# Retention attention and two routed expert layers on one core: border by halves, first expert in sequence, last routing in steps

## The chip, the cores and the metric

One core of a Trainium2 chip runs the whole program in one launch. The metric is the device time of one execution in microseconds (us).

## What is computed

Three layers follow one another on 1536 tokens of 512 values. The reference, cut to what matters:

```python
# attention, B=2, H=8, S=768, D=64
for t in range(S):
    state = gamma * state + outer(k[:, :, t], v[:, :, t])
    y[:, :, t] = scale * einsum('bhd,bhde->bhe', q[:, :, t], state)
# first expert layer, on tokens with x @ w_skip > 0, E=8, F=1024
e_idx = argmax(xc @ w_gate); gate_w = softmax(xc @ w_gate)[e_idx]
out = x; out[do_compute] = xc + gate_w * (relu(xc @ w1[e]) @ w2[e])
# second expert layer, on all tokens, each expert up to its capacity
out[i] = gate_w[i] * (relu(x[i] @ w1[e]) @ w2[e])
```

## The kernel before

**Attention** runs over six chunks of 128 positions, for both sequences (`units`, line 529). `main` (line 661) issues scores, the running state, outputs and, between their steps, one step of routing the chunk before (`sink`, line 423): the logits, the pick of an expert (`pick`, line 282), the row numbers (`numbers`, line 405, on POOL), the tokens' rows turned back (`rows_T`, line 390), written to a table in DRAM (`write_rows`, line 335), their ranks, and one-hot matrices `where` that TensorE sums into `tab`, the table of slots (`to_slots`, line 322). The keys are scaled by decays on POOL (`scale_k`, line 570; `decays`, line 582, prepares the queries' factors `gqc`).

**Weights** come in pieces of 1 MB over SP's queue into five buffers `big` (`load_w`, line 205), in the order of the list `order`. Each is split into a high and a low part of FP32R, `hi` by ACT (line 237) and `lo` by DVE (line 240), and `pump` (line 255) issues a part of a split at each step of the program. The product of two such operands is three matmuls (`mm3`, line 757). Three split weights fit during attention, five after it.

**The border** between attention and experts is `last_chunk` (line 461). The first 128-row block of expert 0, `a0`, is gathered from the table once chunk 4's rows are written; the rows of chunk 5 that belong to it are added by one-hot products (`place`, line 352). Then come the slot sums of chunk 5, the gathers of the other experts' blocks, and the first layer.

**The first expert layer** runs over eight experts with one block each: `layer1` (line 766), then `layer2` of the expert before (line 783), with side steps (`step_side`, line 894) that route each finished block for the second expert layer (`route_b`, line 806): transposes, logits, pick, ranks, slot sums. After expert 7 its routing must be through before the blocks of the second layer can be gathered. Meanwhile block (0, 0) of the second layer, which is known earlier, is computed. The other blocks go in pairs (`pair_layer1`, `pair_layer2`), and `emit_out` (line 860) scales and scatters the results.

The order is written out by hand: each engine executes its instructions in program order, and an instruction that waits holds up all behind it on its engine or queue. PE below is TensorE, DVE VectorE, ACT ScalarE, POOL GpSimd, SP the engine whose queue issues the loads; PEld are PE's loads of the stationary operand.

## Time and profile before

| | us |
|---|---|
| median of 3 runs | 414.49 |
| range of the runs | 414.24 to 416.0 |
| the profiled execution | 413.43 |
| span of its trace | 411.6 |
| PE busy in the span | 381.8 (93%) |
| DVE, ACT, POOL busy | 247.3, 210.0, 119.4 |

The span is from the first to the last instruction; 1.8 us of the execution lie outside it. A wait in the trace is idle time of an engine together with the instruction that released it.

### The profile page before, as it was taken

How to read it: one execution, taken by the hardware profiler on the slowest of the kernel's cores; microseconds unless marked ns; L12 is line 12 of the kernel's file. 1: busy time of each engine (PE TensorE's matmuls, PEld its weight loads, DVE VectorE, ACT ScalarE, POOL GpSimd, SP SyncE). 2: the span in 40 equal slices, each digit the busy share in tenths (PEclk: the TensorE clock that was granted, in tenths of full speed). 3: DMA queues.
4: the chain of work that ended last, by engine and by line, in shares of the span. 5: the costliest groups of instructions: out<-in, count | busy, mean ns of one | idle time of the engine just before them, and what ended most of it. 6: DMA issues, size and time to landing. Idle time of an engine off the chain costs nothing.

```text
span 411.6 us, 6872 instructions
## 1 busy us (share of the span) xinstructions
PE 381.8 (93%) x2665; PEld 311.9 (76%) x2665; DVE 247.3 (60%) x440; ACT 210.0 (51%) x318; POOL 119.4 (29%) x184
## 2 busy tenths in 40 slices
PE   8879999688999999999886999999999999999993
PEld 4768778566767667766554899898989889898982
DVE  4646776549896896896652497274555637364310
ACT  1435553258776677667431665374535556354301
POOL 3665764271044043033034210311304030130202
PEclk8998999989999999999999999999999999999998
DMA  8997965749988887987963287475865657520101
GB/s 292 418 419 279 352 245 148 304 117 352 388 298 335 325 304 285 344 273 287 344 233 91 83 265 262 161 258 204 271 217 182 216 184 231 191 76 2 50 3 39
DMA packets 18336, 95.99 MB, mean 233 GB/s; under 512 B 2481, under 2 KB 2737, under 8 KB 8824
## 3 DMA queue, kind: packets, MB, share of 16 engines
q1 hardware_dynamic: 12068, 80.33, 53.6%
q0 software_dynamic: 3280, 9.76, 7.3%
q10 hardware_dynamic: 2948, 5.39, 3.5%
q8 instruction: 23, 0.38, 0.4%
q14 instruction: 17, 0.14, 0.1%
HBM read 87.03 MB, written 9.48 MB: 234 GB/s over the span
## 4 chain that ended last, share of the span: by engine, by line
PE 66%; DVE 12%; DMA 10%; ACT 6%; issue 5%; POOL 1%; SPq 0%; POOLq 0%; DVEq 0%; ACTq 0%
PE s L759 10%; PE s L761 10%; PE s L760 10%; PE o L761 7%; PE o L759 7%; PE o L760 7%; DVE lo L240 5%; DMA big<-in_w1a_dram 4%; ACT hi L237 4%; PE o L789 2%; DMA table<-rowc 2%; DVE xl L363 2%; PE m L644 2%; DMA wgt<-in_wg_dram 2%; PE m L637 1%
## 5 line engine op out<-in xcount | busy, mean ns | idle before, releaser
L240 DVE TENSOR_TENSOR lo<-big,hi 128x1024 fp32r<-128x1024 f32 (+1 forms) x126 | 145.1, 1184 | 56.0 <-ACT hi L237 55.4
L237 ACT ACTIVATE hi<-big 128x1024 fp32r<-128x1024 f32 (+1 forms) x126 | 121.8, 1014 | 3.5 <-DMA big<-in_w1a_dram 3.5
L759 PE MATMUL o<-hi,hTh 128*128 128x512 f32 x176 | 72.1, 409 | 0.3 <-ACT hTh L362 0.3
L761 PE MATMUL o<-hi,hTl 128*128 128x512 f32 x176 | 70.0, 398 | 1.0 <-DVE hTl L363 1.0
L760 PE MATMUL o<-lo,hTh 128*128 128x512 f32 x176 | 69.7, 396 | 0.0
L761 PE MATMUL s<-xh,lo 128*128 128x256 f32 x224 | 63.4, 283 | 0.0
L760 PE MATMUL s<-xl,hi 128*128 128x256 f32 x224 | 63.4, 283 | 0.0
L759 PE MATMUL s<-xh,hi 128*128 128x256 f32 x224 | 63.4, 283 | 0.0
L865 POOL DMA_INDIRECT out_dram<-y,ixo x16 | 18.2, 1137 | 142.2 <-ACT y L862 121.8
L759 PEld LDWEIGHTS s<-xh,hi 128*128 128x128 f32 x224 | 43.0, 192 | 0.3
L760 PEld LDWEIGHTS s<-xl,hi 128*128 128x128 f32 x224 | 43.0, 192 | 0.3
L761 PEld LDWEIGHTS s<-xh,lo 128*128 128x128 f32 x224 | 43.0, 192 | 0.0
L761 PEld LDWEIGHTS o<-hi,hTl 128*128 128x128 f32 x176 | 33.1, 188 | 9.7 <-DVE hTl L363 1.8
L759 PEld LDWEIGHTS o<-hi,hTh 128*128 128x128 f32 x176 | 33.1, 188 | 7.1 <-ACT hTh L362 0.5
L760 PEld LDWEIGHTS o<-lo,hTh 128*128 128x128 f32 x176 | 33.3, 189 | 6.7
L996 DVE SCALAR_TENSOR_TENSOR hTl<-s,hTh 128x512 fp32r<-128x512 f32 x28 | 19.3, 688 | 31.7 <-ACT hTh L995 31.7
L759 PE MATMUL s<-hi,xh 128*128 128x512 f32 x80 | 35.5, 444 | 2.2 <-ACT xh L362 1.3
L995 ACT ACTIVATE hTh<-s 128x512 fp32r<-128x512 f32 x28 | 16.7, 598 | 40.2 <-PE s L761 40.2
L862 ACT ACTIVATE y<-o,rowc 128x512 f32<-128x512 f32 x15 | 10.3, 689 | 47.2 <-issue 29.4
L761 PE MATMUL s<-hi,xl 128*128 128x512 f32 x80 | 32.1, 401 | 0.8 <-DVE xl L363 0.8
L760 PE MATMUL s<-lo,xh 128*128 128x512 f32 x80 | 31.9, 399 | 0.0
L842 POOL TENSOR_SCALAR rhsb<-m,cs 128x8 bf16<-128x8 bf16 x8 | 2.5, 306 | 85.2 <-DVE se L304 73.3
(151 smaller groups left out, 545.2 us busy)
## 6 DMA issues: line engine op xcount, KB each, us to landing
big<-in_w1a_dram SPq DMA_DIRECT2D x16, 1024.0 KB, 6.6
big<-in_w2a_dram SPq DMA_DIRECT2D x16, 1024.0 KB, 6.8
big<-in_w1b_dram SPq DMA_DIRECT2D x16, 1024.0 KB, 5.4
big<-in_w2b_dram SPq DMA_DIRECT2D x16, 1024.0 KB, 5.0
qk<-in_qkv_dram SPq DMA_DIRECT2D x5, 1024.0 KB, 9.8
big<-in_qkv_dram SPq DMA_DIRECT2D x5, 1024.0 KB, 6.4
table<-rowc ACTq DMA_DIRECT2D x5, 516.0 KB, 7.7
table<-row ACTq DMA_DIRECT2D x8, 258.0 KB, 4.0
```

The source lines that it names most:

```text
L237: nc.scalar.activation(out=hi[:, k], in_=r3[:, k], func=ACTF.Copy)
L240: nc.vector.tensor_tensor(out=lo[:, k], in0=r3[:, k], in1=hi[:, k].bitcast(F32), op=ALU.subtract)
L363: nc.vector.tensor_tensor(out=lo, in0=src, in1=hi.bitcast(F32), op=ALU.subtract)
L644: nc.tensor.matmul(out=o[64 * j:64 * j + 64, 128 * r:128 * r + 128], lhsT=v[:, b, 2 * r + j, :], rhs=pt[c, b][j][:, r, :], start=not c and ...
L759: nc.tensor.matmul(out=acc, lhsT=a[0], rhs=w[0], start=first, stop=False)
L760: nc.tensor.matmul(out=acc, lhsT=a[0], rhs=w[1], start=False, stop=False)
L761: nc.tensor.matmul(out=acc, lhsT=a[1], rhs=w[0], start=False, stop=last)
L789: nc.tensor.matmul(out=acc, lhsT=a[0][:, k % 4, :], rhs=w[:, k % 4, :], start=k == 0, stop=k == FT - 1)
L862: nc.scalar.activation(out=y, in_=acc, func=ACTF.Copy, scale=xs[:, GCOL + 1:GCOL + 2])
L865: new = nc.gpsimd.indirect_dma_start(out=out[:, :], out_offset=bass.IndirectOffsetOnAxis(ap=ix, axis=0), in_=y, in_offset=None, bounds_che ...
L995: nc.scalar.activation(out=hi[:, g:g + 2, :], in_=acc, func=ACTF.Relu)
L996: nc.vector.scalar_tensor_tensor(out=lo[:, g:g + 2, :], in0=acc, scalar=0.0, in1=hi[:, g:g + 2, :].bitcast(F32), op0=ALU.max, op1=ALU.subtract
```

## The change

At load, the first chunk's queries and keys come for both halves, then the values whole, then the keys by token. In attention, splits begin at chunk 2 and are issued in three steps of four, the weights of expert 0's second layer stand right behind those of its first, keys are scaled as part of the scores' step, the decays come one step earlier, and chunk rows are written to the table right after they are turned back. At the border, chunk 5's rows are placed by halves together with `a0`, both sequences' gates are made at once and their rows are written by one DMA on SP's queue; slot sums and gathers move behind the first steps of the first layer. A layer's products of two k's are ordered so that the four with the high part of the tokens come before the two with the low part (`mm3s`). Expert 0's second layer follows its first directly, and expert 1 comes after. Each block's turned tokens come after one step of the layer before, and slot sums in `route_b` come one step later. The last routing is interleaved with steps of two products of the second layer's first block, with its gate ahead of the pick, and the block's second layer then runs whole. The last output block is scaled half by ACT and half by DVE.

```diff
             nc.sync.dma_start(out=qk[:, :, b], in_=qkv[0, :, 0:2, b])
-            nc.sync.dma_start(out=kv[:, 1, b], in_=qkv[0, :, 3, b])
-        nc.sync.dma_start(out=kv[:, 0], in_=qkv[0, :, 2])
+        for i in (1, 0):
+            nc.sync.dma_start(out=kv[:, i], in_=qkv[0, :, 2 + i])
         return qk, kv
 
     grow = a_p.tile([128, 512], F32, name="grow", bufs=1)
...
         add_chunks(w1a, e, "w1a")
-        if e:
-            add_chunks(w2a, e - 1, "w2a")
+        if e != 1:
+            add_chunks(w2a, e - 1 if e else 0, "w2a")
...
             rows_T(xt, rc, 0, psum)
             if c < NCH - 2:
                 yield
             rows_T(xt, rc, 1, psum)
+            write_rows(nc.scalar, rc, B)
             yield
             rk = psum("s", 4)
             ranked(rk, lc[:, 0, :], m.rearrange("p n j -> p (n j)"), cum.rearrange("p a j -> p (a j)"))
             sl = slot(rk, m3, B)
             where = [slots_of(sl, i) for i in bs]
-            write_rows(nc.scalar, rc, B)
             for i in bs:
                 counted(m3[:, i, :])
             yield
...
+            lgs = logits(xt, [0], psum)
             yield
-            lg[0] = logits(xt, [0], psum)
+            picked(0, lgs)
             yield
-            picked(0)
-            rows_T(xt, rc, 0, psum)
-            lg[1] = logits(xt, [1], psum)
+            xr = turned_rows(xt, 0, psum)
             sl = [ranks(0)]
-            picked(1)
+            lgs = logits(xt, [1], psum)
+            nc.scalar.activation(out=rc[:, 0, 0:DM], in_=xr, func=ACTF.Copy)
+            warm(psum("s", 4), 1)
+            picked(1, lgs)
             rows_T(xt, rc, 1, psum)
-            warm(psum("s", 4), 3)
+            warm(psum("s", 4), 1)
             sl.append(ranks(1))
             acc = [psum("m"), psum("m")]
             place(acc, *late[0], True, False)
-            where = [slots_of(sl[b], 0) for b in range(B)]
-            for b in range(B):
-                gates[b]()
-                write_rows(nc.scalar, rc[:, b:b + 1, :], 1)
-            place(acc, *late[1], False, False)
-            for b in range(B):
-                to_slots(where[b], rhs[b][:, 0], 0, 16)
-            nc.vector.tensor_copy(out=ids, in_=tab)
             hi = x_p.tile([128, KT, 128], F32R, tag="xh", name="xh")
             lo = x_p.tile([128, KT, 128], F32R, tag="xl", name="xl")
+            gate(ex, B, 2, rc[:, :, GCOL:GCOL + 2])
+            write_rows(nc.sync, rc, B)
             for g in range(2):
                 ks = slice(2 * g, 2 * g + 2)
+                place(acc, *late[1], False, False, range(KT)[ks])
                 place(acc, a0, ident, False, True, range(KT)[ks])
                 split(acc[g][:, 0:256].rearrange("p (k t) -> p k t", k=2), hi[:, ks], lo[:, ks])
             x0.append((hi, lo))
-            for e in (1, 0, 2, 3):
-                xs1[e] = gather(ids[:, e:e + 1], 1 + NT)
-            for b in range(B):
-                counted(m2[b])
...
+            def gather_all():
+                where = [slots_of(sl[b], 0, sm, "whereb", 2) for b in range(B)]
+                for b in range(B):
+                    to_slots(where[b], rhs[b][:, 0], 0, 16)
+                nc.vector.tensor_copy(out=ids, in_=tab)
+                for e in (1, 0, 2, 3):
+                    xs1[e] = gather(ids[:, e:e + 1], 1 + NT)
+                for b in range(B):
+                    counted(m2[b])
+
+            x0.append(gather_all)
...
-            for g in side[0:1] if c < NCH - 1 else list(side):
+            for g in side[0:1] if c < NCH - 1 else side[::-1]:
...
             if pump and c >= 1 and (c, b) != units[-1]:
-                pump(4, count["turn"] % 3 > 0)
+                pump(4, c >= 2 and count["turn"] % 4 > 0)
...
             scale_q(c, b)
+            if b == 0 and 0 < c < NCH - 1:
+                scale_k(c)
             yield
...
+                if (c, b) == units[-1]:
+                    yield
             for r in range(4):
                 for j in range(2):
...
             o3 = o.rearrange("p (r t) -> p r t", r=4)
-            if (c, b) == units[-1]:
-                nc.vector.tensor_copy(out=xt[c][:, b], in_=o3)
-            else:
-                nc.scalar.activation(out=xt[c][:, b], in_=o3, func=ACTF.Copy)
...
                 yield from scores(c, 1)
+                if c and c + 1 < NCH:
+                    decays(c + 1)
                 if c == 0 and pump:
                     derived_late()
...
                 yield from state(c)
-            elif c + 1 < NCH:
-                decays(c + 1)
             if c + 1 < NCH:
                 yield from scores(c + 1, 0)
-                if c + 1 < NCH - 1:
-                    scale_k(c + 1)
             if c:
                 yield from outs(c, 1)
...
 
+    def mm3s(acc, pairs, first, last):
+
+        todo = [(a[0], w[i]) for a, w in pairs for i in range(2)] + [(a[1], w[0]) for a, w in pairs]
+        for i, (a, w) in enumerate(todo):
+            nc.tensor.matmul(out=acc, lhsT=a, rhs=w, start=first and i == 0, stop=last and i == len(todo) - 1)
+            if i % 2 and i < len(todo) - 1:
+                yield
+
...
         h = m_p.tile([128, FF], F32, tag="h", name="h", bufs=1)
         for j in range(2):
             acc = psum("s", 2)
             w = wt[kind, e, j]
-            for k in range(KT):
-                mm3(acc, at_k(x, k), at_k(w, k), k == 0, k == KT - 1)
-                if k == 1:
+            for k in (0, 2):
+                for _ in mm3s(acc, [(at_k(x, i), at_k(w, i)) for i in (k, k + 1)], k == 0, k == 2):
+                    if fine:
+                        yield
+                if not k:
+                    if j and parts is not None:
+                        parts.append(turned(h, 0, "hT"))
                     yield
-                if k == 2 and j and parts is not None:
-                    parts.append(turned(h, 0, "hT"))
             used((kind, e, j)) if done_with(kind, e) else None
...
             write_rows(nc.scalar, r2.unsqueeze(1), 1)
         nc.gpsimd.tensor_tensor(out=cumb, in0=cumb, in1=m, op=ALU.subtract)
-        yield from idle(2 if e < E - 1 else 1)
+        yield from idle(3 if e < E - 1 else 1)
         to_slots(where, rhs, 8, 8)
         yield
...
         y = m_p.tile([128, DM], F32, tag="y", name="y")
-        nc.scalar.activation(out=y, in_=acc, func=ACTF.Copy, scale=xs[:, GCOL + 1:GCOL + 2])
+        n = DM // 2 if shared else DM
+        nc.scalar.activation(out=y[:, 0:n], in_=acc[:, 0:n], func=ACTF.Copy, scale=xs[:, GCOL + 1:GCOL + 2])
+        if shared:
+            nc.vector.tensor_scalar(out=y[:, n:DM], in0=acc[:, n:DM], scalar1=xs[:, GCOL + 1:GCOL + 2], scalar2=None, op0=ALU.mult)
         ix = sm.tile([128, 1], I32, tag="ixo", name="ixo")
...
-    for e in range(E):
-        h = run(layer1(x, "w1a", e))
+    h0 = []
+    first = layer1(x, "w1a", 0, h0)
+    next(first)
+    x0[1]()
+    step_side()
+    h = run(first)
+    xs1[4] = gather(ids[:, 4:5], 1 + NT)
+    second = layer2(h0, "w2a", 0)
+    next(second)
+    h0.append(turned(h, 1, "hT"))
+    step_side()
+    next(second)
+    step_side()
+    x = turned(xs1[1], 0, "x")
+    acc = run(second)
+    then_route(0, acc, 1, 1)
+    for e in range(1, E):
+        first = layer1(x, "w1a", e)
+        if e == 1:
+            for _ in range(2):
+                next(first)
+                step_side()
+            x = turned(xs1[2], 0, "x")
+        h = run(first)
...
-        if e == 0:
-            next(turn)
-        x = run(split_T(xs1[e + 1] if e + 1 < E else a0, KT, "x"))[0]
-        if e:
-            acc = run(layer2(hT.pop(e - 1), "w2a", e - 1))
-            then_route(e - 1, acc, 2, 2)
+        if e > 1:
+            second = layer2(hT.pop(e - 1), "w2a", e - 1)
+            next(second)
+            step_side()
+            x = turned(xs1[e + 1] if e + 1 < E else a0, 0, "x")
...
+            acc = run(second)
+            then_route(e - 1, acc, *((2, 1) if e < E - 1 else (0, 0)))
         hT[e] = run(turn)
-    acc = run(layer2(hT.pop(E - 1), "w2a", E - 1))
-    last = then_route(E - 1, acc, 0, 1)
+    second = layer2(hT.pop(E - 1), "w2a", E - 1)
+    for i in range(FT // 2):
+        next(second)
+        pieces[0] = i < 2
+        step_side()
+    acc = run(second)
+    last = route_b(E - 1, xs1[E - 1], acc, 0, 0)
+    next(last)
 
...
     h0 = []
-    h = run(layer1(x, "w1b", 0, h0))
+    first = layer1(x, "w1b", 0, h0, True)
+    for i in range(1, 13):
+        next(first)
+        if i % 3 == 0:
+            step_side()
+        if i in (2, 4, 5, 9, 12):
+            next(last)
+    try:
+        next(first)
+    except StopIteration as stop:
+        h = stop.value
+    nc.vector.tensor_copy(out=ids_b, in_=tab[:, 8:24])
+    for e, j in ((0, 1), (1, 0), (1, 1), (2, 0), (2, 1)):
+        load_block(e, j)
+    second = layer2(h0, "w2b", 0)
+    next(second)
     h0.append(turned(h, 1, "hT"))
-    second = layer2(h0, "w2b", 0)
...
+    acc = run(second)
     while side:
         step_side()
     x = turned(xs2[0, 1], 0, "x")
-    acc = run(second)
+    pieces[0] = 1
...
                 if c:
-                    emit_out(xs2[e, j], acc[j])
+                    emit_out(xs2[e, j], acc[j], e == E - 1 and j > 0)
```

POOL's order in chunk 1: `big_86` are the keys, `rhs` the row numbers, `qk` the queries, `cum` the running counts. Before:

```order
L591 TENSOR_TENSOR qk<-qk,gqc 128x512
L409 TENSOR_SCALAR rhs<-m,cs 128x2x16
L410 TENSOR_TENSOR rhs<-m,his 128x2x16
L575 TENSOR_TENSOR big_86<-big_86,cs 128x512 x2
L591 TENSOR_TENSOR qk<-qk,gqc 128x512
L416 TENSOR_TENSOR cum<-cum,m 128x32 x2
L584 TENSOR_TENSOR gqc<-cs 128x512
L591 TENSOR_TENSOR qk<-qk,gqc 128x512
```

And now:

```order
L604 TENSOR_TENSOR qk<-qk,gqc 128x512
L588 TENSOR_TENSOR big_86<-big_86,cs 128x512 x2
L416 TENSOR_SCALAR rhs<-m,cs 128x2x16
L417 TENSOR_TENSOR rhs<-m,his 128x2x16
L604 TENSOR_TENSOR qk<-qk,gqc 128x512
L597 TENSOR_TENSOR gqc<-cs 128x512
L423 TENSOR_TENSOR cum<-cum,m 128x32 x2
L604 TENSOR_TENSOR qk<-qk,gqc 128x512
```

The keys' two products stand ahead of the row numbers, and the decays' product `gqc` ahead of the counts `cum`.

PE's order at the border, where `oh` are the one-hot rows of chunk 5 (one buffer for each sequence), `a0` the gathered block and `m` the two accumulators. Before, down to the first slot sums, and then from the last of them to the first layer:

```order
L356 MATMUL m_1118<-oh_1077,rowc2_109 128x128 x2
L356 MATMUL m_1119<-oh_1077,rowc2_109 128x128 x2
L356 MATMUL m_1118<-oh_1116,rowc2_109 128x128 x2
L356 MATMUL m_1119<-oh_1116,rowc2_109 128x128 x2
L327 LDWEIGHTS where_1124
L327 MATMUL tab_120<-rhs_1054,where_1124 128x16
```

```order
L327 MATMUL tab_120<-rhs_1095,where_1126 128x8
L356 MATMUL m_1118<-cs_84,a0_106 128x128 x2
L356 MATMUL m_1119<-cs_84,a0_106 128x128 x2
L759 MATMUL s_1195<-hi_393,xh_1153 128x512
```

And now:

```order
L360 MATMUL m_1116<-oh_1068,rowc2_108 128x128 x2
L360 MATMUL m_1117<-oh_1068,rowc2_108 128x128 x2
L360 MATMUL m_1116<-oh_1114,rowc2_108 128x128 x2
L360 MATMUL m_1116<-cs_84,a0_105 128x128 x2
L360 MATMUL m_1117<-oh_1114,rowc2_108 128x128 x2
L360 MATMUL m_1117<-cs_84,a0_105 128x128 x2
L779 MATMUL s_1160<-hi_441,xh_1122 128x512
L779 MATMUL s_1160<-lo_442,xh_1122 128x512
L779 MATMUL s_1160<-hi_441,xh_1122 128x512
L779 MATMUL s_1160<-lo_442,xh_1122 128x512
L779 MATMUL s_1160<-hi_441,xl_1123 128x512 x2
L331 LDWEIGHTS whereb_1167
L331 MATMUL tab_119<-rhs_1044,whereb_1167 128x16
```

The slot sums `tab` have moved behind six products of the first layer, and `a0` is placed into the first accumulator before the second one is filled.

DVE's order at the last routing: `row` is the finished block, `prb` to `whereb` belong to the ranks of the block before, `mx` to `m` to the pick. Before:

```order
L240 TENSOR_TENSOR lo<-big_88,hi 128x1024 x2
L810 SCALAR_TENSOR_TENSOR row_1189<-o,rowc_107 128x512
L848 TENSOR_TENSOR prb<-t,m 128x8
L850 TENSOR_REDUCE slb<-prb 128x1
L852 TENSOR_SCALAR whereb<-iota,slb 128x257
L287 TENSOR_REDUCE mx<-t 128x1
L290 TENSOR_TENSOR d<-t,mx 128x8
L296 SCALAR_TENSOR_TENSOR t_117<-d,rmb 128x8
L298 TENSOR_REDUCE tm<-t_117 128x1
L300 TENSOR_TENSOR m<-t_117,tm 128x8
L304 TENSOR_REDUCE se<-ex 128x1
L306 TENSOR_SCALAR sf<-se 128x1
```

And now:

```order
L873 TENSOR_TENSOR prb<-t,m 128x8
L875 TENSOR_REDUCE slb<-prb 128x1
L877 TENSOR_SCALAR whereb<-iota,slb 128x257
L834 SCALAR_TENSOR_TENSOR row_1154<-o,rowc_106 128x512
L287 TENSOR_REDUCE mx<-t 128x1
L290 TENSOR_TENSOR d<-t,mx 128x8
L297 SCALAR_TENSOR_TENSOR t_116<-d,rmb 128x8
L310 TENSOR_REDUCE se<-ex 128x1
L312 TENSOR_SCALAR sf<-se 128x1
L313 RECIPROCAL row_1154<-sf 128x1
L301 TENSOR_REDUCE tm<-t_116 128x1
L303 TENSOR_TENSOR m<-t_116,tm 128x8
```

The two `lo` pieces no longer stand ahead of `row`, the ranks of the block before do, and `se` to the reciprocal (the gate) stand ahead of `tm` and `m`.

## Rows read from the trace of the kernel before

**Rows 1.** Stages: span, busy us (count) of PE, PEld, DVE, ACT, POOL; PEclk, DMA share, GB/s.

```profile
12.00:28.00 16.00, 14.40 (x213) 11.84 (x209) 6.78 (x21) 6.79 (x16) 10.67 (x17) 1.00 1.01 418
240.00:402.00 162.00, 162.00 (x1047) 147.11 (x1046) 84.65 (x91) 77.03 (x102) 29.52 (x36) 1.00 0.49 170
```

**Rows 2.** Waits of PE over the whole span: us in total, times, longest.

```profile
PE t L738 <- DMA rowc<-table,ids_b: 2.6, 1, 2.6
PE tab L327 <- DVE whereb L852: 2.1, 6, 0.5
PE tab L327 <- DVE where L420: 2.0, 3, 0.7
PE s L375 <- DVE p L607: 2.0, 1, 2.0
PE t L824 <- DVE row L810: 1.9, 2, 1.5
PE m L356 <- DMA a<-table,ids: 1.8, 1, 1.8
...
PE u L620 <- POOL big L575: 1.3, 2, 1.0
PE s L759 <- ACT xh L362: 1.3, 1, 1.3
PE t L738 <- ACT h L779: 1.1, 1, 1.1
PE o L761 <- DVE hTl L363: 1.0, 1, 1.0
PE s L759 <- DVE xl L363: 0.9, 1, 0.9
...
PE s L761 <- DVE xl L363: 0.8, 1, 0.8
```

**Rows 3.** The same columns as Rows 1, two stretches at a lower granted clock.

```profile
31.80:35.30 3.50, 3.50 (x42) 3.38 (x42) 2.86 (x13) 2.27 (x7) 1.98 (x3) 0.53 1.03 424
83.40:86.60 3.20, 3.17 (x8) 2.49 (x9) 1.23 (x1) 0.47 (x1) 2.51 (x3) 0.50 0.29 83
```

**Rows 4.** Loads issued from 8.2 to 8.3 us: KB each, us to landing.

```profile
big<-in_qkv_dram SPq DMA_DIRECT2D x1, 1024.0 KB, 7.9
```

**Rows 5.** Chain of waits around 27.7 us: start, us, what.

```profile
11.58 16.12 DMA big<-in_w1a_dram
```

**Rows 6.** DVE in order of time, 56 to 72 us: start, us, instruction.

```profile
59.56 0.19 DVE L401 TENSOR_TENSOR pr<-s,m 128x32 f32<-128x32 f32 x1 [1.04 <-PE s L318]
...
60.01 1.41 DVE L420 TENSOR_SCALAR where<-iota,sl 128x257 bf16<-128x257 f32 x2
...
69.83 0.62 DVE L420 TENSOR_SCALAR where<-iota,sl 128x257 bf16<-128x257 f32 x2
```

**Rows 7.** POOL in order of time, 59.5 to 62 us.

```profile
60.10 1.16 POOL L584 TENSOR_TENSOR gqc<-cs 128x512 f32<-128x512 f32 x1
```

**Rows 8.** Chain of waits from the last attention chunk to the first layer.

```profile
69.35 6.62 DMA table<-rowc
...
76.83 4.47 DMA a<-table,ids
...
83.43 0.79 PE s L759
```

**Rows 9.** DMAs issued from 59.5 to 64 us: KB, us to landing.

```profile
table<-rowc ACTq DMA_DIRECT2D x1, 516.0 KB, 4.3
```

**Rows 10.** PE in order of time, 76 to 80 us: the slot sums.

```profile
78.64 0.88 PE L327 MATMUL tab<-rhs,where 128*128 128x16 bf16 x8
```

**Rows 11.** DVE in order of time, 205 to 210 us.

```profile
206.56 2.36 DVE L240 TENSOR_TENSOR lo<-big,hi 128x1024 fp32r<-128x1024 f32 x2
208.83 0.74 DVE L810 SCALAR_TENSOR_TENSOR row<-o,rowc 128x512 f32<-128x512 f32 x1
```

**Rows 12.** Costliest groups on the page: the output scaling on ACT.

```profile
L862 ACT ACTIVATE y<-o,rowc 128x512 f32<-128x512 f32 x15 | 10.3, 689 | 47.2 <-issue 29.4
```

More of the change, by code (lines that the diff above doesn't have):

```diff
@@ L941, in load_block @@
         xs2[e, j] = gather(ids_b[:, 8 * j + e:8 * j + e + 1])
[L943 to L953 removed]
+    h0 = []
+    first = layer1(x, "w1b", 0, h0, True)
+    for i in range(1, 13):
+        next(first)
+        if i % 3 == 0:
+            step_side()
+        if i in (2, 4, 5, 9, 12):
[8 more added lines that the diff above has]
+    second = layer2(h0, "w2b", 0)
+    next(second)
     h0.append(turned(h, 1, "hT"))
[L955 to L958 removed]
+    acc = run(second)
     while side:
@@ L1021 @@
     h = run(layer1(x, "w1b", 0, h0))
+    second = layer2(h0, "w2b", 0)
+    next(second)
+    h0.append(turned(h, 1, "hT"))
+    step_side()
     x = pair_T(1)
-    h0.append(turned(h, 1, "hT"))
     flag = overflow(ct)
-    acc = run(layer2(h0, "w2b", 0))
+    acc = run(second)
     emit_out(xs2[0, 1], acc)
```

97 lines of the change are left out of this document (50 added, 47 removed).

## The prediction, made before the changed kernel ran

> **What bounds the kernel now.** I read the table of stages first. In the long last stage, 240 to 402 us, PE is busy for all 162.00 us [rows 1]; the change reorders nothing there, and nothing is to be had. Earlier it is busy 14.40 of 16 us in the stretch from 12 to 28 us [rows 1]. PE is the bound with gaps in it, so the second view is the list of what PE waited for: twelve entries carry the argument, from 2.6 us for the last gather down to 0.8 us [rows 2]. The third view is the granted clock. Over 31.80 to 35.30 us it is 0.53 and over 83.40 to 86.60 us 0.50, so at or near the lower of its two levels (1.2 of 2.4 GHz) [rows 3]; PE had waited 2.0 us ahead of the first stretch and 1.8 and 0.9 us ahead of the second [rows 2]. Each gap that goes therefore counts once as wait and may count again as clock. The sum is made against the profiled execution, 413.43 us, of which 411.6 is span; the median of the runs, 414.49, lies 1.1 above it, and I carry that over.
>
> **The change part by part.** *Load order.* The same bytes come in one DMA fewer; the next thing that is needed is no later. Costed at nothing.
>
> *Keys ahead of row numbers.* PE waits 1.3 us in two places for POOL's scaled keys [rows 2]. In the new order the two products stand ahead of the row numbers, which wait for DVE's pick. Their input is there: the load issued just after 8.2 us took 7.9 us, so it landed at about 16.1 [rows 4], before POOL comes to it. The row numbers start later by the two products, but the slot sums that use them come several PE steps later. Gain 1.3 us, between 0 and 1.3.
>
> *Splits from chunk 2.* The first weight piece landed 16.12 us after its issue at 11.58, at 27.7 [rows 5]. ACT waited for it in order, DVE behind ACT, and PE's logits behind DVE's product: 2.0 us [rows 2]. From chunk 2 on the piece is there when ACT comes to it. The stretch at half speed that followed goes too: 3.50 us of work at 0.53 would take 1.9 at the full clock, a gain of 1.6 [rows 3]. Together 3.6 us, at least the 2.0.
>
> *Decays one step earlier.* PE waits three times, 2.0 us in all, for `where` [rows 2]. That pair of DVE instructions takes 1.41 us while POOL runs the decays' product of 1.16 us beside it, and 0.62 where POOL does not [rows 6, 7]. In the new order the product runs before the ranks, in a stretch in which DVE had 1.04 us of idle time ahead of `pr` [rows 6]. At 0.62 `where` ends inside PE's scores and the wait is gone: 2.0 us. The Trainium skill, page "SBUF — State Buffer", section "Who interferes with whom", says that a DVE instruction with two SBUF inputs and a GpSimd instruction that reads SBUF block each other fully, in order of issue. By that rule the product now blocks the weights' `lo` in its new place; what it could shift is the rival on `where` below.
>
> *Border.* The chain to the first layer is: rows of chunk 4 to the table, 6.62 us; gather of `a0`, 4.47 us; placing and splitting, first layer at 83.43 [rows 8]. The write was issued together with weight loads. In the changed program SP's queue stands, at that point, behind the write of chunk 5's rows, so the next weight loads come after it. The nearest row is the same write one chunk earlier, without fresh loads behind it: 4.3 us [rows 9]. So `a0` comes 2.3 us earlier, between 0 and 2.3; I take the upper end, as it is the same size and the same distance from a weight load. The Trainium skill, page "DMA: Bandwidth & Descriptors", section "Anatomy of one DMA", gives 2.0 us and bytes over 436 GB/s per DMA; for 516 KB that is an estimate of 3.2 us, and the border would gain 1.1 more. The trace has 4.3 and that is used.
> PE is there in time: it waited 1.8 us for `a0` [rows 2], after 0.88 us of slot sums that now come later [rows 10], so it arrives 2.7 us early and keeps a wait of about 0.4. Behind `a0` the wait of 0.9 for the low part goes [rows 2], since four products with the high part now come first; the second half's placing comes in for it, which I put at 0.6. Net 0.3. The slot sums cost PE 0.6 (0 to 0.88) inside the layer. With PE's waits shorter, the half-speed stretch after the border should go: 3.20 us at 0.50, 1.6 us [rows 3]; it may stay, so 0 to 1.6. Border in all: 2.3 + 0.3 − 0.6 + 1.6 = 3.6 us.
>
> *Expert 0's layers in sequence.* PE waited 1.3 and 0.8 us for expert 1's turned tokens [rows 2]. Now the second layer of expert 0 lies between, 24 products, and the gather has that time to land. Gain 2.1. The price is on DVE: the splits of expert 0's and 1's weights stand ahead of `row` and of the first pick. The nearest row is the wait for `row`, 0.4 and 1.5 [rows 2]; I count two waits, 1.5 us, against the 0.4 there is now: −1.1 (0 to −2.6).
>
> *Slot sums one step later.* Six waits for `whereb`, 2.1 us [rows 2], between 0.2 and 0.5 each; one more step of PE is over a microsecond. Gain 2.1.
>
> *Expert 7 and the last routing.* The turn of expert 7's hidden rows moves between steps of the layer before: 1.0 us [rows 2]. Then three waits are attacked: 1.5 for `row`, which stood behind two `lo` pieces of 2.36 us [rows 11]; 1.1 for the hidden rows; 2.6 for the last gather [rows 2]. The routing is now stepped at two products, and a whole second layer of 24 products comes after the gather's issue, which covers the 3 to 5 us of a gather [rows 8]. New waits: `row` stands behind the ranks of the block before (0.9, between the two waits known for it), the last slot sums follow their `whereb` closely (0.5, the longest of the six), and the next block's tokens are turned right before they are used (0.7; now 0.8 to 1.3 for such a wait) [rows 2]. So 5.2 − 2.1 = 3.1 us, from 0 to 5.2.
>
> *Last output by halves.* One scaling takes 0.69 us [rows 12]; halves on two engines save about 0.3. The general path, which is not executed, and the write of expert 6's rows, which PE does not wait for, cost nothing.
>
> **Sum.** 1.3 + 3.6 + 2.0 + 3.6 + 2.1 − 1.1 + 2.1 + 1.0 + 3.1 + 0.3 = 18.0 us. 413.4 − 18.0 = 395.4 for an execution like the profiled one, 396.5 for the median. All of it is idle or half-speed time of PE; no product of the layers is added or removed.
>
> **Rivals.** (1) *The loads take the place of the waits.* From 12 to 28 us the DMA engines are fully busy, 1.01 of their time [rows 1]. If the first chunks then wait for their own loads, 1.3 and 3.6 are lost: 401.4. Against it: what chunk 1 needs stood in the queue ahead of the weights and landed at 16.1 [rows 4].
> (2) *The border stays as long.* The write shares the engines with loads still in flight, and takes 6.62 again [rows 8]; PE then idles longer than now and the clock falls again: 2.3 + 1.6 lost, 400.4.
> (3) *The last routing only trades its waits.* If the new ones are as long as the old, 3.1 is lost: 399.6.
> (4) *`where` meets another POOL instruction.* The queries' product now follows close behind; if it starts first, the 2.0 stays: 398.5.
> (5) *Splits come late: slower.* Loads for experts 1 and 2 stand behind the table write on SP, and two first layers follow each other. If this leaves the split of each later expert behind, each pays what the one late piece cost here, 2.0 us of wait and 1.6 of clock [rows 2, 3]: seven times 3.6 is 25.2, 421.7. It decides from five experts on. Against it: five split weights fit from the border on, and there is no such wait in the experts now [rows 2].
>
> **Chances and range.** Forecast 0.53, rivals (1) 0.12, (2) 0.15, (3) 0.10, (4) 0.08, (5) 0.02. The forecast's own range is 393 to 399. The low end is the sum with half of the new waits gone and the page's faster write; the high end takes in (1) to (4) one at a time: 391.5 to 402.5. A measurement of this kernel tells about 0.5% (2 us) from no change; every case but (5) is beyond that on the faster side. Two rivals together are still 10 us faster. Faster 0.96, the same 0.02, slower 0.02.
>
> **What would show it.** The trace after should have no wait of PE for `big`, `p` and `where` in attention, and the full clock through it from 15 us on; the write of chunk 4's rows landing in under 5 us; the first layer starting at about 73 us (83.4 less 7 and 3), at the full clock; no wait for expert 1's tokens; `whereb` gone from the list; after expert 7 three waits of under 1 us each. The prediction is wrong if the attention's chunks wait for loads, if ACT waits for weight pieces among the experts, or if waits of more than 4 us in sum that are not named here appear on PE.

## The result and the profile after

| | before | changed |
|---|---|---|
| median, us (4 runs each on one chip) | 415.25 | 400.49 |
| range of these runs | 414.24 to 416.42 | 399.98 to 401.93 |
| the profiled execution | 413.43 | 399.98 |
| span of its trace | 411.6 | 398.2 |
| PE busy in the span | 381.8 | 377.3 |

The ratio is 0.9649 (95% interval 0.9609 to 0.969). The prediction was 396.5 us with a range of 391.5 to 402.5: the sign and the range hold, but of the 18.0 us of the sum only 13.4 arrived. Two of the prediction's own signs of being wrong came up as well: ACT waits 2.10 us for a weight piece among the experts, and PE has more than 4 us of waits that were not named (both below). What PE waits for now (us in total, times, longest), to be set beside [rows 2]:

```profile
PE t L848 <- DVE row L834: 6.9, 8, 2.7
PE s L538 <- DVE zb L113: 1.4, 1, 1.4
PE s L779 <- DVE xl L367: 0.9, 1, 0.9
PE s L779 <- ACT xh L366: 0.7, 1, 0.7
PE t L317 <- DVE m L303: 0.6, 1, 0.6
PE s L317 <- DVE m L303: 0.6, 1, 0.6
PE tab L331 <- DVE whereb L877: 0.5, 1, 0.5
PE t L750 <- ACT h L801: 0.4, 1, 0.4
...
```

Nearly every wait that was to go is gone: `big`, `p`, the first block `a`, expert 1's tokens, the last gather; and `where` has no line any more. One new line leads the list: the finished block's `row`, 6.9 us in eight places, against 1.9 in two. Where the time went by stages is read from the first products of the stages (start, duration, instruction). Before (the first layer's start is in [rows 8]):

```profile
14.39 0.64 PE L375 MATMUL s<-xt,wgt 128*32 128x256 f32 x8
...
206.19 0.79 PE L759 MATMUL s<-hi,xh 128*128 128x512 f32 x1
...
226.69 0.47 PE L759 MATMUL s<-hi,xh 128*128 128x512 f32 x1
```

And after:

```profile
15.88 0.64 PE L379 MATMUL s<-xt,wgt 128*32 128x256 f32 x8
...
74.57 0.50 PE L779 MATMUL s<-hi,xh 128*128 128x512 f32 x1 [0.93 <-DVE xl L367]
...
196.25 0.48 PE L779 MATMUL s<-hi,xh 128*128 128x512 f32 x1
...
213.32 0.50 PE L779 MATMUL s<-hi,xh 128*128 128x512 f32 x1 [0.66 <-ACT xh L366]
```

| stage | before | after | gain | by the prediction |
|---|---|---|---|---|
| start to the first logits | 14.39 | 15.88 | −1.5 | 0 |
| first logits to the first layer | 69.04 | 58.69 | 10.4 | 9.5 |
| first layer to the second layer's first block | 122.76 | 121.68 | 1.1 | 5.1 |
| that block, with the last routing | 20.50 | 17.07 | 3.4 | 3.1 |
| the rest | 184.9 | 184.9 | 0 | 0.3 |

In the last column, attention and border up to the first layer are 1.3 + 3.6 + 2.0 + 2.3 + 0.3; the experts are 2.1 − 1.1 + 2.1 + 1.0 and the border's clock less the slot sums inside the layer, 1.6 − 0.6. So two questions are left: the 4.0 us that the experts did not give, and the 1.5 us of the start.

The granted clock in three stretches of the changed kernel (span, busy us and counts by engine, clock, DMA share, GB/s):

```profile
8.00:16.00 8.00, 7.64 (x92) 7.02 (x94) 3.86 (x10) 2.18 (x5) 3.89 (x7) 0.60 1.03 415
32.00:36.00 4.00, 4.00 (x57) 3.51 (x56) 2.64 (x10) 3.45 (x8) 3.17 (x6) 1.00 1.00 414
74.00:84.00 10.00, 9.43 (x52) 7.63 (x53) 6.61 (x9) 6.53 (x10) 5.13 (x5) 1.00 0.96 332
```

Both stretches of [rows 3] are at 1.00 now, the two terms of 1.6 us. The stretch from 8 to 16 us, at 0.60, was at 0.79 before; it belongs to the question of the start.

### The profile page after: what moved, and what is told of

It reads as the page before. It is cut to its first block, busy times and chain, and to the rows that moved or that the text cites. A ratio compares the mean times of both kernels' runs of the same rounds, so it can differ in the third digit from the quotient of the medians.

```text
span 398.2 us, 6863 instructions
## 1 busy us (share of the span) xinstructions
PE 377.3 (95%) x2664; PEld 310.6 (78%) x2664; DVE 243.5 (61%) x437; ACT 210.7 (53%) x319; POOL 119.0 (30%) x184
## 5 line engine op out<-in xcount | busy, mean ns | idle before, releaser
L773 PE MATMUL o<-hi,hTl 128*128 128x512 f32 x112 | 44.4, 396 | 0.0
L779 PE MATMUL s<-hi,xh 128*128 128x512 f32 x80 | 34.3, 429 | 1.6 <-DVE xl L367 0.9
L888 ACT ACTIVATE y<-o,rowc 128x512 f32<-128x512 f32 (+1 forms) x15 | 10.1, 675 | 46.7 <-issue 29.4
L779 PE MATMUL s<-hi,xl 128*128 128x512 f32 x80 | 25.1, 394 | 0.0
L773 PEld LDWEIGHTS o<-hi,hTl 128*128 128x128 f32 x112 | 21.1, 188 | 5.1
```

Source lines behind the costliest of these rows:

```text
L773: nc.tensor.matmul(out=acc, lhsT=a[1], rhs=w[0], start=False, stop=last)
L779: nc.tensor.matmul(out=acc, lhsT=a, rhs=w, start=first and i == 0, stop=last and i == len(todo) - 1)
L888: nc.scalar.activation(out=y[:, 0:n], in_=acc[:, 0:n], func=ACTF.Copy, scale=xs[:, GCOL + 1:GCOL + 2])
```

## Experiments

All kernels but x9 are the changed one with one edit. Each was timed beside the kernel before; the ratio to that, the median and the span of the profile are given. Since the start varies (below), I also give the span less the time of the first logits: 382.3 for the changed kernel, 382.4 when it ran again.

> The changed kernel once more, unaltered, so that the runs beside it are read against one on the same chip. Every theory: about 400 us, span 397 to 398.5, PE's waits for the row 6 to 7 us with the longest, at expert 1, from 1.2 to 2.7 us (that one followed the time of the weights' landing in the runs so far); the first logits between 15.0 and 15.95 us.

x5: ratio 0.9619 (0.9561 to 0.9678), 400.0 us, span 398.6, first logits at 16.16, a little later than expected, the waits for `row` 6.8. The changed kernel repeats.

### The start: x1 and x9

x1 restores the load order of the first chunk:

```diff
             nc.sync.dma_start(out=qk[:, :, b], in_=qkv[0, :, 0:2, b])
-        for i in (1, 0):
-            nc.sync.dma_start(out=kv[:, i], in_=qkv[0, :, 2 + i])
+            nc.sync.dma_start(out=kv[:, 1, b], in_=qkv[0, :, 3, b])
+        nc.sync.dma_start(out=kv[:, 0], in_=qkv[0, :, 2])
```

> The changed kernel with the loads of the first chunk in their old order (values by halves, keys last); all else as changed. In the changed kernel the first logits of attention start at 15.9 us, against 14.4 before: the constants for the masks landed 0.5 us later, PE waited 0.31 and 0.36 us, and the granted clock stayed at 0.50 until about 14 us instead of 11.4. Theory (the load order costs this): the first logits are back at 14.4 to 14.6, the clock rises at about 11.5, and 1.5 us come off: span 396.7, about 399.0 us. Rival (the start differs by chance, or by what POOL and DVE do there): first logits at 15.9 again, span 398.2, 400.5 us.

Measured: 0.9678 (0.9604 to 0.9752), 399.58 us, span 396.8, first logits at 15.13. The span is what the theory said, but by the first logits it stands between the two. x2 and x3, which keep the new load order, had them at 15.05 and 15.33. So the unaltered kernel before was profiled again.

> The kernel before once more, unaltered, for a second profile of its start. In five profiles of the changed kernel and its variants the first logits stood between 14.7 and 16.2 us, in the one profile of before at 14.4; two kinds of start were seen, one at the full clock and one with two gaps of PE and the lower clock from 8 to 14 us. Theory (the start differs from execution to execution, and the load order of the change has no part in it): first logits anywhere from 14.4 to 16.2, span 411 to 413.5. Rival (the old load order always starts at 14.4, and the changed one loses about 1 us): 14.3 to 14.5, span 411.6.

One execution, 411.62 us, span 409.8. PE in order of time:

```profile
14.89 0.72 PE L598 MATMUL s<-qk 64*128 64x128 f32 x8 [1.03 <-DMA qk<-in_qkv_dram]
15.53 0.64 PE L375 MATMUL s<-xt,wgt 128*32 128x256 f32 x8
...
30.16 0.64 PE L375 MATMUL s<-xt,wgt 128*32 128x256 f32 x8 [0.98 <-DVE p L607]
...
81.72 0.79 PE L759 MATMUL s<-hi,xh 128*128 128x512 f32 x1 [0.93 <-DVE xl L363]
```

The first logits come at 15.53 here, 1.1 later than in the other execution of the same kernel, so the start differs from execution to execution and my theory on the load order falls. The 1.1 is a wait of PE for a load (1.03), which no profile of the changed kernel or its variants has. In these twelve profiles the first logits lay between 14.66 and 16.25: at 15.88 to 16.25 in the four in which the granted clock over 8 to 16 us was 0.57 to 0.60 (the changed kernel's first profile is one), at 14.66 to 15.33 in the eight in which it was 1.00. What puts an execution into one group was not found. The third row says more: chunk 2's logits came at 30.16 against 30.02 in the first execution, with a wait for `p` of 0.98 where there it was 2.0 [rows 2]. So before the change a late start was absorbed here by the wait for the first weight piece; the changed kernel has no such wait. In its profiles, and in those of x1 to x6, x11 and x12, the first layer starts 58.7 us behind the first logits each time, whenever these came, and a late start reaches the end.

The last row bears on the stage table. In this execution attention, from the first logits to the first layer, took 66.19 us, not 69.04: the wait of 0.98 was followed by the full clock (1.00 over 24 to 36 us), and the half-speed stretch at 31.8 us [rows 3] is not there. Against this execution the stage gained 7.5 us, not 10.4. The 1.6 us at half speed behind the border is in both (0.50 over 81.7 to 85 us here).

### The experts: x2, x3, x4

The waits for `row` lie here (PE in order of time, changed kernel):

```profile
114.67 0.66 PE L848 MATMUL t<-cs,row 128*128 128x128 f32 x4 [2.74 <-DVE row L834]
...
129.64 0.65 PE L848 MATMUL t<-cs,row 128*128 128x128 f32 x4 [0.82 <-DVE row L834]
...
144.63 0.66 PE L848 MATMUL t<-cs,row 128*128 128x128 f32 x4 [0.20 <-DVE row L834]
...
159.57 0.66 PE L848 MATMUL t<-cs,row 128*128 128x128 f32 x4 [0.78 <-DVE row L834]
...
174.51 0.66 PE L848 MATMUL t<-cs,row 128*128 128x128 f32 x4 [0.17 <-DVE row L834]
...
190.09 0.66 PE L848 MATMUL t<-cs,row 128*128 128x128 f32 x4 [1.35 <-DVE row L834]
```

The rows come 15.0 us apart, as they did before the change, although the six waits for `whereb` are gone. What `row` stands behind (ACT, then DVE, in order of time):

```profile
107.17 1.06 ACT L237 ACTIVATE hi<-big 128x1024 fp32r<-128x1024 f32 x1 [2.10 <-DMA big<-in_w2a_dram]
...
111.59 2.36 DVE L240 TENSOR_TENSOR lo<-big,hi 128x1024 fp32r<-128x1024 f32 x2 [0.37 <-ACT hi L237]
113.87 0.74 DVE L834 SCALAR_TENSOR_TENSOR row<-o,rowc 128x512 f32<-128x512 f32 x1
...
118.80 0.17 DVE L287 TENSOR_REDUCE mx<-t 128x1 f32<-128x8 f32 x1 [3.00 <-PE t L859]
...
125.44 3.48 DVE L240 TENSOR_TENSOR lo<-big,hi 128x1024 fp32r<-128x1024 f32 x3
128.85 0.74 DVE L834 SCALAR_TENSOR_TENSOR row<-o,rowc 128x512 f32<-128x512 f32 x1
```

At expert 1 ACT waited 2.10 us for a weight piece, so the low pieces on DVE were late and `row` behind them. At the next one DVE went from the pick (`mx`, 118.80) to `row` (128.85) with hardly a pause, 10.05 us, and had waited 3.0 us for the pick's input before. The row, the transposes, the logits, the pick, the low pieces and the next row form a circle. The kernel before went round the same one (DVE in order of time):

```profile
127.98 0.17 DVE L287 TENSOR_REDUCE mx<-t 128x1 f32<-128x8 f32 x1 [3.08 <-PE t L835]
...
137.99 0.74 DVE L810 SCALAR_TENSOR_TENSOR row<-o,rowc 128x512 f32<-128x512 f32 x1
```

That is 10.0 us from the pick to the row, behind a wait of 3.1. PE's idle time there was booked on `whereb`, now it is booked on `row`; the period stayed at 15.0.

x2 issues the slot sums one step earlier again, counted from the ranks:

```diff
-        yield from idle(3 if e < E - 1 else 1)
+        yield from idle(2 if e < E - 1 else 1)
```

> The changed kernel with the slot sums of a block one step earlier again, as before the change; nothing else differs. The prediction gave their move 2.1 us. Theory (the experts go round a closed circle: DVE's pick, eight low pieces, the finished block's row, PE's transposes and logits, DVE's pick; it takes 15.0 us, and a wait of PE that is not on it is paid back at the next wait for the row): PE waits for the slots' one-hot rows again, some 2 us in all, its waits for the row shrink from 6.9 to about 5, and the span stays at 398.2, within 0.5. Rival (the prediction's term): 2.1 us more, span 400.3, 402.6 us.

Measured: 0.9657 (0.9591 to 0.9723), 399.25 us, span 397.2, less the first logits 382.15. Two waits of PE over the whole span:

```profile
PE t L848 <- DVE row L834: 5.1, 7, 1.4
PE tab L331 <- DVE whereb L877: 1.7, 2, 1.1
```

The run does not put all the old waits back: at experts 2 to 5 PE does not wait for `whereb`, since the ranks stand a step earlier than before the change, too ((2, 2) became (2, 1) there). It waits 1.1 at expert 0, 1.7 with the last routing's (0.5 in the changed kernel), and 1.8 less for the row; the time is the same within 0.2. At experts 2 and 4 the waits for the row are 0.77 and 0.74, as in the changed kernel. So the run tests one wait: the 1.1 at expert 0 is repaid at the next wait for `row`, at expert 1 (1.24 for 2.74), where the row comes late because of the late weight piece. The six waits that the prediction counted, at experts 1 to 6, it does not test.

x3 puts the transposes of the finished block one step later on PE:

```diff
-            then_route(e - 1, acc, *((2, 1) if e < E - 1 else (0, 0)))
+            then_route(e - 1, acc, *((3, 1) if e < E - 1 else (0, 0)))
```

> The changed kernel with the transposes of each finished block (experts 1 to 5) one step later in PE's order, so that PE has about 1.4 us more work before it needs the row. Theory (the circle through DVE sets the period of 15.0 us): the wait only stands elsewhere; the rows follow each other at 15.0 us as now, span 398.2, within 0.7. Rival (the row is merely late for PE by a fixed time, and more work ahead of its use covers it): waits of 0.8, 0.2, 0.8 and 0.2 us go and 1.4 of the 2.7 at expert 1, together 3.4: span 394.8, 397.1 us.

Measured: 0.9612 (0.9547 to 0.9678), 397.83 us, span 396.2, less the first logits 380.9. The waits for `row` at experts 2 to 5 are gone, and the one at expert 1 is 1.34. DVE in order of time:

```profile
117.81 1.23 DVE L240 TENSOR_TENSOR lo<-big,hi 128x1024 fp32r<-128x1024 f32 x1 [2.59 <-ACT hi L237]
118.95 0.16 DVE L287 TENSOR_REDUCE mx<-t 128x1 f32<-128x8 f32 x1
...
127.47 0.74 DVE L834 SCALAR_TENSOR_TENSOR row<-o,rowc 128x512 f32<-128x512 f32 x1
```

My expectation, no gain, fell. PE comes to the rows of experts 1 to 5 14.40 us apart on the average now (114.08 to 171.69), against 14.96 in the changed kernel (114.67 to 174.51). The 0.56 is little more than the 0.49 that PE waited for each of the rows 2 to 5 there. The rows show why the circle is no objection: the pick, too, is issued a step later, one low piece moved ahead of it into time that DVE had spent waiting, and from the pick to `row` it is 8.5 us, not 10.05. So this run does not tell the circle from the rival, which named the waits that go. Of 3.0 us less waiting for `row` (6.9 to 3.9) only 1.4 showed: at expert 6 the wait for `row` became 1.76, and behind it the clock was 0.82 over 186.4 to 196 us, some 1.7 us lost.

x4 moves two low pieces behind the row. While `hold` is set, in the last two steps of the layer, no piece is issued; afterwards each step issues one more until they are caught up:

```diff
+            if e < E - 1:
...
+                hold[0] = True
             acc = run(second)
+            hold[0] = False
             then_route(e - 1, acc, *((2, 1) if e < E - 1 else (0, 0)))
```

> The changed kernel with two of the low pieces that stand ahead of a finished block's row on DVE moved behind it, for experts 1 to 5; the pieces are caught up in the next two steps. Nothing else moves on DVE. Theory (the row waits in DVE's queue behind these pieces, and they close the circle of 15.0 us): the wait for the row goes at these five places, 2.7 + 0.8 + 0.2 + 0.8 + 0.2 = 4.7 us, the rows follow each other at about 14.5 us, PE's own work; span 393.5 to 395, about 396.5 us. Rival (loads or splits set the period): the weights' pieces are now late by two, PE waits for weights or ACT for loads instead, and the span stays at 398 or rises.

Measured: 0.966 (0.9592 to 0.9728), 399.6 us, span 397.7, less the first logits 381.75. A wait of PE, and ACT in order of time:

```profile
PE t L857 <- ACT x2t L853: 3.7, 2, 1.9
...
127.07 2.00 ACT L237 ACTIVATE hi<-big 128x1024 fp32r<-128x1024 f32 x2
128.96 0.59 ACT L853 ACTIVATE x2t<-t 128x512 f32<-128x512 f32 x1
```

The waits for `row` went as expected (1.9 in three places are left), but 3.7 came back under another name: the copy `x2t` of the turned rows stands on ACT behind the `hi` halves of the pieces that are caught up, and behind the first of these waits, of 1.84 us, the clock was 0.91 over 125 to 144 us. The gain is 0.6. A low piece is not moved alone.

### The terms that held: x8, x10, x7, x11

x8 issues splits from chunk 1 in steps of three again:

```diff
-                pump(4, c >= 2 and count["turn"] % 4 > 0)
+                pump(4, count["turn"] % 3 > 0)
```

> The changed kernel with the splits of attention issued from chunk 1 on in steps of three again, as before the change. Theory (the first weight piece lands at about 27 us, and ACT, DVE and PE wait for it in their order): PE's wait of about 2 us ahead of chunk 2's logits is back, with some 3 us at the lower clock behind it, so 3 to 4 us more in attention; the first layer starts at 77 to 78 us, and of this up to 2 us may be given back at expert 1, where the splits are further on; span 399.5 to 402. Rival (with the other edits of attention ACT comes to the piece later, and the wait is hidden): first layer at 74 to 74.6 us, span 397 to 398.

Measured: 0.9752 (0.9693 to 0.981), 405.44 us, span 404.0, first layer at 78.67.

```profile
PE s L379 <- DVE p L620: 2.8, 1, 2.8
...
32.00:36.00 4.00, 4.00 (x43) 3.87 (x43) 2.48 (x12) 2.65 (x7) 2.59 (x4) 0.50 0.99 412
```

The wait for `p` and the lower clock behind it are back; the span is above the 402 expected. From the first logits to the first layer it takes 64.0 us, 5.3 more than in the changed kernel (3.6 were costed; the medians differ by 5.4). PE comes to the wait earlier now (it was 2.0 before), and the piece does not land earlier for it; and the stretch at half speed lasts from 31 to 37 us, where before it lasted from 32 to 35. At expert 1 hardly anything is given back (2.42 of wait for `row`), and behind that wait the clock was 0.65 over 118.4 to 122 us, so that the next row came 16.5 us later, not 15.0: less the first logits the span is 389.3, 7.0 more.

x10 issues the decays' product one step later again:

```diff
                 yield from scores(c, 1)
-                if c and c + 1 < NCH:
-                    decays(c + 1)
...
+            elif c + 1 < NCH:
+                decays(c + 1)
             if c + 1 < NCH:
```

> The changed kernel with the decays' product issued where it stood before, one step later, beside the ranks. Theory of the prediction (DVE's pair of slot rows takes 1.41 us beside that product and 0.62 without, and PE waits for it): the pair takes 1.3 to 1.5 us in chunks 1 to 4 again, PE's waits for it are back, 1.5 to 2 us in all; span 399.5 to 400.6 against 398.2 to 398.6, about 401.8 us. Rival (the new place of the keys on POOL keeps the product away from the pair, or PE has slack there now): the pair takes 0.62, no wait, span 398.2 to 398.6.

Measured: 0.9729 (0.9684 to 0.9773), 402.59 us, span 398.6 with first logits at 14.88. The pair on DVE in x10, then in the changed kernel:

```profile
34.00 1.41 DVE L427 TENSOR_SCALAR where<-iota,sl 128x257 bf16<-128x257 f32 x2
```

```profile
34.69 0.62 DVE L427 TENSOR_SCALAR where<-iota,sl 128x257 bf16<-128x257 f32 x2
```

PE waits 2.2 us for `where` in four places, and attention from the first logits to the first layer takes 61.1 us for 58.7. Less the first logits the span is 383.7, 1.4 more than the changed kernel's: of the 2.4 about 1 is gone at expert 1, where the wait for `row` was 1.36; since that wait was 1.70 to 2.74 in the profiles with the same order up to there, how much of this is the edit's doing is not shown. By the medians the run is 2.1 to 2.6 slower. The term of 2.0 holds up to the first layer; how much of it reaches the end is between 1.4 and 2.6.

x7 writes the last chunk's rows over ACT's queue, so that SP goes on with weight loads:

```diff
-            write_rows(nc.sync, rc, B)
+            write_rows(nc.scalar, rc, B)
```

> The changed kernel with the rows of attention's last chunk written over ACT's queue, not SP's, so that SP issues the next weight loads beside the write of chunk 4's rows, as before the change. Theory of the prediction (the write of chunk 4's rows takes 4.3 us where no weight load stands beside it and 6.6 where one does): the gather of the first block is held up by about 2 us, the first layer starts 1 to 2 us later against attention's end, and PE waits for that block; but the weights land earlier, and the wait for the row at expert 1 falls by up to 2; span 397 to 399. Rival (the write's length has another cause): gather and first layer stand where they are, only the weights come earlier, span 395.5 to 397.

Measured: 0.9734 (0.9671 to 0.9796), 403.91 us, span 401.6, first layer at 77.21, less the first logits 385.35. The gather of the first block in x7 (KB, us to landing), and the wait that follows:

```profile
a<-table,ids POOLq DMA_INDIRECT x1, 7.1
...
PE m L360 <- DMA a<-table,ids: 2.0, 1, 2.0
```

The same gather in the changed kernel:

```profile
a<-table,ids POOLq DMA_INDIRECT x1, 3.6
```

The wait is the one expected (2.0 us, the first layer 2.3 later), the span, 3.0 above x5's, is not: 397 to 399 was expected. The gather left POOL 3.7 us after the write's issue in x7 as in x5 (63.79 to 67.51, 63.70 to 67.44), so the write took no longer. The gather did, 7.1 us for 3.6, beside two weight loads issued at 65.90 and 67.66. The edit does not put the old place of the loads back: before the change one was issued right behind the write (69.40 behind 69.35), here 2.1 us later. So x7 prices a load beside the gather, and says nothing on a load beside the write. The earlier weights took the wait at expert 1 from 2.59 to 1.92, but behind it the clock was 0.60 over 116.5 to 120 us, where in x5 it had stayed at 1.00, and 1.5 us were lost.

x11 puts the last routing back, with the code of the kernel before (cut):

```diff
-    last = route_b(E - 1, xs1[E - 1], acc, 0, 0)
-    next(last)
+    last = then_route(E - 1, acc, 0, 1)
...
-    first = layer1(x, "w1b", 0, h0, True)
+    h = run(layer1(x, "w1b", 0, h0))
...
     second = layer2(h0, "w2b", 0)
-    next(second)
-    h0.append(turned(h, 1, "hT"))
-    acc = run(second)
+    for _ in range(FT // 2 - 1):
+        next(second)
+        step_side()
```

> The changed kernel with the last routing as before the change: steps of six products, the pick ahead of the gate, the gathers issued in the block's second layer, and that layer split by the wait for the gather. Theory of the prediction (the new stepping gains 3.1, taking 5.2 of waits away and adding 2.1): 2.5 to 4 us more behind expert 7, PE waits 2 to 3 us for the last gather and 1 to 1.5 for the hidden rows; span 400.7 to 402.5, about 403.5 us. Rival (the gather is covered in either order because the block before is further on): span within 1 us of 398.4.

Measured: 0.9871 (0.9826 to 0.9917), 408.76 us, span 406.4, less the first logits 391.2. Waits of PE:

```profile
PE t L848 <- DVE row L834: 9.7, 8, 4.0
PE t L750 <- DMA rowc<-table,ids_b: 2.6, 1, 2.6
PE t L750 <- ACT h L801: 1.8, 1, 1.8
```

The gather's 2.6 and the hidden rows' wait are back as expected, and on top of that expert 7's `row` costs 3.98, with a lower clock behind it (0.79 over 200 to 208 us) and again behind the gather (0.64 over 217.8 to 222 us). The span is 4 us above the range expected. In this surrounding the new stepping is worth 8 us. What it gained against the kernel before is the 3.4 of the stage table.

### A faster version: x6 and x12

x6 is x3 with two low pieces moved behind expert 6's `row`:

```diff
-                for _ in range(2):
+                for i in range(2):
                     next(second)
+                    hold[0] = i > 0
                     step_side()
                     next(turn)
...
             acc = run(second)
+            hold[0] = False
```

> The changed kernel with the transposes of each finished block one step later for experts 1 to 5 (as in the run before), and for expert 6 two low pieces moved behind its row on DVE and caught up in the next two steps. Theory (each wait for a row is a place where the row stands behind weight pieces on DVE; where the place allows it, either more work of PE ahead of it or fewer pieces ahead of it takes the wait away): the wait at expert 6, 1.8 us, falls to under 0.3, and the stretch at the lower clock that followed it is gone (about 1.5 us); span 393 to 394, about 396 us. Rival (the pieces that are caught up hold up the copy of the turned rows on ACT or the pick on DVE, as they did when two pieces were moved at every expert): the wait only changes its name, span 396.

Measured: 0.956 (0.9507 to 0.9612), 396.41 us, span 394.1, less the first logits 379.2. The wait at expert 6 went and the lower clock with it; 1.70 us came as a wait for the pick, which stood on DVE behind the pieces that were caught up. x12 catches them up behind the last pick, and puts expert 1's transposes two steps later:

```diff
-            then_route(e - 1, acc, *((3, 1) if e < E - 1 else (0, 0)))
+            catch[0] = int(e < E - 1)
+            then_route(e - 1, acc, *((4 if e == 2 else 3, 1) if e < E - 1 else (0, 0)))
...
         if i % 3 == 0:
+            catch[0] = int(i == 6)
             step_side()
```

> The version with the transposes one step later, and two steps later for expert 1, whose row waits for late weights; for expert 6 two low pieces are moved behind its row, and they are caught up only after the last pick. Theory (what is left of the waits for the row, 1.3 us at expert 1, and the 1.7 us for the pick that the two caught-up pieces caused at expert 6, go; no other wait takes their place): span 391.5 to 393, about 394 us. Rival (the weights of the second layer are then split too late, or the late weights of expert 1 show at the next wait): span 394, or above.

Measured: 0.9526 (0.9493 to 0.9559), 394.42 us, span 392.1, less the first logits 377.1. PE's waits that are left behind attention:

```profile
PE tab L334 <- DVE whereb L880: 1.7, 2, 1.2
...
PE t L851 <- DVE row L837: 0.8, 2, 0.6
...
143.00:158.00 15.00, 14.98 (x91) 11.21 (x90) 12.41 (x22) 11.53 (x17) 2.46 (x6) 1.00 0.89 339
158.00:173.00 15.00, 15.00 (x79) 10.67 (x79) 11.57 (x22) 9.89 (x16) 2.46 (x6) 1.00 0.92 323
```

The waits for `row` are down from 6.9 to 0.8 us, and PE is busy practically without a gap from 143 to 173 us (14.98 and 15.00 of 15 us). Two waits for `whereb` came in their place: 0.45 at expert 1, and 1.22 behind a caught-up piece in the last routing. The median is 5.6 us under that of x5 and 6.1 under the first runs of the changed kernel.

## Why the prediction was right, and where it was not

**Keys ahead of row numbers, splits, decays, border** (9.5 of the sum up to the first layer; measured 10.4 against the execution that the sum was made from, 7.5 against x9). The waits for `big`, `p`, `where` and `a` are gone, both stretches at half speed too. That the gain comes so near the price holds for the profiled pair only: 1.6 of the price is a half-speed stretch that the second execution of the kernel before did not have. x8 and x10 show the mechanisms of the splits and of the decays by putting them back; no run puts the keys' order back. The pair `where` took 1.41 us beside POOL's product and 0.62 without [rows 6, 7], and x10 moved the 1.41 with the product. The Trainium skill, page "SBUF — State Buffer", section "Who interferes with whom", says that a DVE instruction with two SBUF inputs contends with a GpSimd instruction that reads SBUF. The trace goes that way, though `where` reads one tensor and one scalar per partition; whether the page's rule takes that for two inputs no run shows. In its new place the product costs nothing on PE. The border's gain came. The gather was issued 7.5 and 7.7 us behind the write of chunk 4's rows in the two profiles of before, and 3.7 to 4.9 in the twelve of the changed kernel and its variants; the gather itself took 4.5 and 4.0, and takes 3.6 (7.1 in x7). So most of the gain lies on the write, as predicted. x7 adds that loads beside the gather lengthen it. Why the write took 6.62 us before was not tried. The wait of 0.9 for the low part, which was to go, is still there (0.93): the layer's first product is released by the second half's `xl`, although it reads the high part. Why was not tried.

**Expert 0's layers in sequence** (2.1 − 1.1). Expert 1's tokens are not waited for any more, and the new waits were 0.23 for expert 0's `row` and 0.60 for the pick, less than the 1.5 counted. The price left out expert 1's `row`, which waits for late weights (next paragraph). No run puts the old sequence back.

**Slot sums one step later and expert 7's turn** (2.1 + 1.0): this is the step that failed. It counted six waits for `whereb` and one for the hidden rows as gone and asked nothing of what PE then runs into. It ran into `row`: 2.74, 0.82, 0.20, 0.78, 0.17 and 1.35 us at experts 1 to 6, 6.1 in sum, none of which the sum had. At experts 2 to 5 (2.0 of it) the period of 15.0 us on either side shows that the waits for `whereb` were worth nothing by themselves; that it is the circle that sets this period is read from the rows, and x3 could not tell it from its rival. At expert 1 (2.7 of it) the row stood behind low pieces that were late because ACT waited for a load: rival (5) had that lateness, priced for all experts or none. Earlier loads (x7, 1.92) and earlier splits (x8, 2.42) did not take it away; why the piece comes late was not tried. x3, x6 and x12 show that the waits for `row` are real time. The prediction had named the low pieces ahead of `row` [rows 11], but only for the last block. 6.1 of new waits, less the 2.1 that the other terms of this stage gave beyond their price, is the 4.0 that is missing.

**The last routing** (3.1; 3.4 measured). The three new waits were counted at 0.9, 0.5 and 0.7; they are 0.61, 0.46 and 0.66.

**Load order and last output.** Costed at 0 and 0.3. The start was 1.5 later in the profiled pair and differs by as much among the profiles of the changed kernel and its variants; no part of it could be pinned on the load order. The last output's 0.3 can't be seen in the stage table.

## What to carry to other kernels

A wait that is removed counts only up to the next wait of the same engine: look at what the next shared instruction stands behind, and whether the wait lies on the circle that sets the period. In an in-order queue, count for each short instruction on the circle what is issued ahead of it on every engine it passes through; moving filler work away from it on one engine puts the other half of that filler in front of something else. A wait on a load that lands at a fixed time can hide variation ahead of it, and removing it brings that variation to the end. A stretch at the lower clock in one profile is that execution's until a second profile shows it too: a sum that counts it may be right for the one and wrong for the other.

## What the runs showed of the hardware

An indirect gather of 128 rows took 3.6 or 3.7 us in eleven profiles, with no load issued in the 8 us before it, and 7.1 in x7, where two loads of 1 MB were issued 1.6 us ahead of it and right behind it. The length of a wait alone does not tell what the granted clock does behind it. At expert 1 the clock stayed at 1.00 behind 2.74 us (the changed kernel) and 2.59 us (x5), and fell behind 1.92 us (x7, 0.60 over 116.5 to 120 us) and 2.42 us (x8, 0.65 over 118.4 to 122 us). At the start it was 0.60 over 8 to 16 us with waits of only 0.31 and 0.36 us ahead. Why is open.
